# First products of two feed-forward layers by seven block products, with their input operands kept in DRAM

## The chip, the cores and the metric

The program runs on one core of a Trainium2 chip. The metric is the device time of one execution in microseconds (us); lower is better. Names used for the engines: PE is TensorE (matrix products into the eight banks of PSUM), PEld its weight loads, DVE is VectorE, ACT is ScalarE, POOL is GpSimd, SP is the engine that issues nearly all DMAs here, in one queue in program order.

## The reference

```python
def _attn_ref(q, k, v):                      # 4 batches, 8 heads, 576 tokens, 64 wide
    scores = scale * np.matmul(q, k.transpose(0, 1, 3, 2))
    ...                                      # heads 0-3: window of 32; heads 4-7: every 32nd key
    return np.matmul(attn, v).astype(np.float32)
def _moe_ref(x, w_in, w_out):                # x: 2304 x 512, w_in: 512 x 2048, w_out: 2048 x 512
    h = x @ w_in
    g = h * np.clip(h + 3.0, 0.0, 6.0) / 6.0
    return (g @ w_out).astype(np.float32)
def _moe2_ref(x, w_in, w_out):               # the same shapes, with g = h * tanh(softplus(h))
    ...
```

Attention is followed by the two layers, each on the output of the one before. The weights are given as 64-bit floats. Both layers have a first product (h = x w_in) and a second one (g w_out), of the same size.

## The kernel before, in words

**Precision.** Every FP32 operand is split into a high and a low part; a product is three matmuls (`mm3`: low weights by high data, high by low, high by high; lines 801 to 803).

**Tiles.** Everything is kept transposed: 512 features are four chunks of 128 partitions (`xh[kc]`, `xl[kc]`: high and low parts of the layer's input), tokens lie along the columns. The 2304 tokens are cut into blocks of 512, 512, 512, 256 and 512 (`BLOCKS`), the 2048 hidden features of a layer into 16 chunks of 128, and these into three groups (`GROUPS`). A step is one chunk of hidden features on one block: 4 x 3 matmuls into one bank (h), the activation out of the bank (ACT `t`, in the first layer also DVE `t`), the split into `gh` (ACT, line 332) and `gl` (POOL, line 867), then 4 x 3 matmuls into four banks (y), which collect over the steps of a group. After a group, y is added to a sum in SBUF (DVE, line 905). After the last group of layer 1 the sum is split into `xh`, `xl` again; after the last of layer 2 it goes out.

**Weights** come by DMA as 64-bit words (`raw`, 512 KB each, 64 of them) and are decoded on DVE and ACT in `decode` (lines 749 to 790), ahead of their use.

**Attention** runs in 16 pairs (4 batches x 4 pairs of heads). A pair is scores (PE, line 569), softmax (DVE, POOL, ACT), transposes (PE, lines 636 and 638), and values (PE, line 675). Pair p of a batch gives chunk p of the features. A step needs the batches that its tokens lie in.

**Order.** `Plan` is a list scheduler that runs when the program is built: every operation has a cost, a due time and a set of engines that can do it, and the result is one fixed order for each engine. Until 60 us it also puts in matmuls on zeros (line 929), to keep PE at work. While attention runs, the layers' first group is interleaved with it.

Of the kernel before, what the change touches and what calls it, by code (L numbers as in the profile page):

```python
# [31 lines left out]
BLOCKS = (512, 512, 512, 256, 512)  # L32

GROUPS = ((4, 6, 6), (6, 5, 5))

LAST_WALK = (0, 1, 2, 4, 3)


SLOTS = 8
EARLY_SLOTS = 6  # L40
EARLY_SUMS = 2

N_RAW, N_WA, N_WM, N_T, N_G = 3, 3, 2, 4, 4
N_QKV, N_E, N_PT = 2, 4, 2

# [5 lines left out]
    "att": (0, 1, 2, 3),  # L51
    "y": (4, 5, 6, 7),
    "h0": (0, 1, 2, 3),
    "h1": (0, 1, 2),
    "y0": (4, 5, 6, 7, 3, 2),
    "y1": (4, 5, 6, 7, 3),
# [5 lines left out]
START, FIRST_PACE = 42731, 3854  # L62
UNIT = 1354
MASKS_DUE = 1000

SOON = 54
# [4 lines left out]
HALF_PACE = 7747  # L71
EARLY_W, EARLY_G, EARLY_X = 9802, 9863, 14382


BIAS = {"act": -442, "dve": 4000, "pool": 0}
FIRST_BIAS = {"act": 3541, "dve": 4000, "pool": 0}
BIAS_FROM = 29872
# [11 lines left out]
LEAD = 0.8883  # L89
# [207 lines left out]
def mm3_ns(n):  # L297

    return 3 * (n + 32) / 2.4
# [7 lines left out]
def attention_then_two_ffns(ctx, tc, qkv, masks, wts, out):  # L307
# [13 lines left out]
    N = max(BLOCKS)  # L321

    blocks = [(sum(BLOCKS[:j]), n) for j, n in enumerate(BLOCKS)]
    assert sum(BLOCKS) == NT and all(sum(g) == NF for g in GROUPS)

# [15 lines left out]

    w_t = [pool.tile([P, 2, DM], F32R, name=f"w{k}") for k in range(2 * EARLY_SLOTS)]
# [3 lines left out]
    gh_t = [pool.tile([P, N], F32R, name=f"gh{k}") for k in range(N_G)]  # L346
    gl_t = [pool.tile([P, N], F32R, name=f"gl{k}") for k in range(N_G)]

    pool.tile([P, 8], F32, name="gap")
    raw_t = [pool.tile([P, DM], U64, name=f"raw{k}") for k in range(N_RAW)]  # L350
    wa_t = [pool.tile([P, DM], F32, name=f"wa{k}") for k in range(N_WA)]
    wm_t = [pool.tile([P, DM], F32, name=f"wm{k}") for k in range(N_WM)]
    all_t = pool.tile([P, N_T, N], F32, name="t")
    t_t = [all_t[:, k] for k in range(N_T)]

    early_ys = pool.tile([P, EARLY_SUMS, KC, N], F32, name="y")
    ys = [early_ys[:, j] for j in range(EARLY_SUMS)]

# [12 lines left out]
    sums, words = (x.rearrange(how) for x, how in ((early_ys, "p j a n -> p (j a n)"), (all_t, "p k n -> p (k n)")))  # L371
# [18 lines left out]
    class Record:  # L390
        pass

    steps = []
    for m in range(2):
        for g, n in enumerate(GROUPS[m]):
            walk = LAST_WALK if (m, g) == (1, len(GROUPS[1]) - 1) else range(len(blocks))
# [608 lines left out]
```

## Time and profile before

| | |
|---|---|
| median of 3 runs | 879.99 us (878.77 to 880.93) |
| the profiled execution: its own time | 879.24 us |
| the profiled execution: span of its trace | 877.4 us, mean granted PE clock 0.991 |
| PE, DVE, ACT, POOL busy | 98%, 50%, 35%, 32% of the span |
| moved by DMA | 57.12 MB |

The span is what the trace covers; 1.84 us of the execution's own time lie outside it. Busy shares are means over the span; matmuls overlap one another in the pipeline, so the time between their starts tells more than their durations.

### The profile page before, as it was taken

How to read it: one execution, taken by the hardware profiler on the slowest of the kernel's cores; microseconds unless marked ns; L12 is line 12 of the kernel's file. 1: busy time of each engine (PE TensorE's matmuls, PEld its weight loads, DVE VectorE, ACT ScalarE, POOL GpSimd, SP SyncE). 2: the span in 40 equal slices, each digit the busy share in tenths (PEclk: the TensorE clock that was granted, in tenths of full speed). 3: DMA queues.
4: the chain of work that ended last, by engine and by line, in shares of the span. 5: the costliest groups of instructions: out<-in, count | busy, mean ns of one | idle time of the engine just before them, and what ended most of it. 6: DMA issues, size and time to landing. Idle time of an engine off the chain costs nothing.

```text
span 877.4 us, 15050 instructions
## 1 busy us (share of the span) xinstructions
PE 857.9 (98%) x6326; PEld 715.6 (82%) x6326; DVE 440.9 (50%) x788; ACT 309.3 (35%) x581; POOL 279.9 (32%) x244
## 2 busy tenths in 40 slices
PE   5899999999999999999999999999999999999998
PEld 2577888888888988888888888898888898888887
DVE  5688868899321588942268960007881114110011
ACT  2566765542222233323333432334422222222221
POOL 4544542322222222334442532222322223222221
PEclk7999999999999999999999999999999999999999
DMA  8846542223000022300002220001320000010012
GB/s 263 250 141 212 156 127 93 77 92 98 22 1 1 25 73 72 96 25 1 1 25 96 72 96 1 1 1 55 114 97 1 1 1 1 0 49 25 25 48 72
DMA packets 19495, 57.12 MB, mean 65 GB/s; under 512 B 2916, under 2 KB 5604, under 8 KB 19428
## 3 DMA queue, kind: packets, MB, share of 16 engines
q1 hardware_dynamic: 18768, 56.01, 19.9%
q8 instruction: 49, 0.80, 0.4%
q10 hardware_dynamic: 660, 0.16, 0.1%
q14 instruction: 18, 0.15, 0.0%
HBM read 51.45 MB, written 4.72 MB: 64 GB/s over the span
## 4 chain that ended last, share of the span: by engine, by line
PE 93%; DMA 3%; ACT 1%; POOL 1%; DVE 1%; issue 0%; SPq 0%; ACTq 0%; POOLq 0%
PE bank L801 30%; PE bank L802 30%; PE bank L803 30%; DMA v<-in_qkv_dram 2%; PE bank L675 2%; PE bank L569 1%; PE bank L636 1%; DMA mk_str<-in_masks_dram 1%; ACT v L535 0%; ACT pt L332 0%; POOL mk_str L492 0%; POOL v L537 0%; PE bank L638 0%; POOL e L627 0%; PE bank L929 0%
## 5 line engine op out<-in xcount | busy, mean ns | idle before, releaser
L867 POOL TENSOR_TENSOR gl<-t,gh 128x512 fp32r<-128x512 f32 (+1 forms) x160 | 204.0, 1275 | 532.6 <-ACT gh L332 460.2
L801 PE MATMUL bank<-gh,w 128*128 128x512 f32 (+1 forms) x640 | 237.8, 372 | 0.0
L801 PE MATMUL bank<-xh,w 128*128 128x512 f32 (+1 forms) x640 | 237.2, 371 | 0.1
L802 PE MATMUL bank<-xl,w 128*128 128x512 f32 (+1 forms) x640 | 236.0, 369 | 0.0
L803 PE MATMUL bank<-xh,w 128*128 128x512 f32 (+1 forms) x640 | 235.8, 368 | 0.0
L802 PE MATMUL bank<-gl,w 128*128 128x512 f32 (+1 forms) x640 | 235.8, 368 | 0.0
L803 PE MATMUL bank<-gh,w 128*128 128x512 f32 (+1 forms) x640 | 235.6, 368 | 0.0
L801 PEld LDWEIGHTS bank<-xh,w 128*128 128x128 f32 x640 | 120.7, 189 | 21.2 <-DVE w L790 0.4
L802 PEld LDWEIGHTS bank<-xl,w 128*128 128x128 f32 x640 | 120.8, 189 | 20.1
L803 PEld LDWEIGHTS bank<-xh,w 128*128 128x128 f32 x640 | 120.6, 188 | 20.2
L801 PEld LDWEIGHTS bank<-gh,w 128*128 128x128 f32 x640 | 120.6, 188 | 20.2
L803 PEld LDWEIGHTS bank<-gh,w 128*128 128x128 f32 x640 | 120.5, 188 | 20.3
L802 PEld LDWEIGHTS bank<-gl,w 128*128 128x128 f32 x640 | 120.6, 189 | 19.0
L905 DVE TENSOR_TENSOR y<-bank,y 128x512 f32<-128x512 f32 (+1 forms) x80 | 49.5, 636 | 170.6 <-PE bank L803 170.3
L820 ACT ACTIVATE t<-bank 128x512 f32<-128x512 f32 (+1 forms) x80 | 44.5, 556 | 240.0 <-PE bank L803 239.9
L332 ACT CAST gh<-t 128x512 fp32r<-128x512 f32 (+1 forms) x160 | 92.7, 580 | 60.0 <-DVE t L812 39.4
L812 DVE SCALAR_TENSOR_TENSOR t<-t,bank 128x512 f32<-128x512 f32 (+1 forms) x80 | 50.5, 632 | 124.5 <-ACT t L809 124.2
L809 ACT ACTIVATE t<-bank 128x512 f32<-128x512 f32 (+1 forms) x80 | 44.5, 556 | 144.6 <-PE bank L803 144.2
L778 DVE TENSOR_SCALAR wa<-wa 128x512 uint32<-128x512 uint32 x64 | 38.8, 607 | 107.7 <-ACT w L332 107.0
L332 ACT CAST w<-wa 128x512 fp32r<-128x512 f32 x64 | 39.7, 621 | 47.6 <-DVE wa L772 24.7
L772 DVE SCALAR_TENSOR_TENSOR wa<-raw,wa 128x512 uint32<-128x512 uint32 x64 | 54.7, 855 | 0.5
L786 DVE SCALAR_TENSOR_TENSOR wm<-wm,raw 128x512 f32<-128x512 uint32 x64 | 49.7, 776 | 0.1
(53 smaller groups left out, 535.1 us busy)
## 6 DMA issues: line engine op xcount, KB each, us to landing
raw<-in_wts_dram SPq DMA_DIRECT2D x64, 512.0 KB, 3.6
qk<-in_qkv_dram SPq DMA_DIRECT2D x14, 576.0 KB, 4.9
v<-in_qkv_dram SPq DMA_DIRECT2D x14, 432.0 KB, 4.9
out_dram<-y SPq DMA_DIRECT2D x16, 256.0 KB, 2.0
y<-in_qkv_dram SPq DMA_DIRECT2D x2, 576.0 KB, 8.2
out_dram<-y SPq DMA_DIRECT2D x4, 128.0 KB
v<-in_qkv_dram SPq DMA_DIRECT2D x14, 32.0 KB, 4.8
y<-in_qkv_dram SPq DMA_DIRECT2D x1, 432.0 KB
```

What stands on the lines that cost most here:

```text
L332: nc.scalar.copy(out, src)
L772: lambda: nc.vector.scalar_tensor_tensor(ai, high, 0xC0000000, ai, ALU.bitwise_and, ALU.bitwise_or),
L778: lambda: nc.vector.tensor_scalar(ai, ai, 0xFF800000, None, ALU.bitwise_and), [o], lock=("dve",),
L786: lambda: nc.vector.scalar_tensor_tensor(rest, resti, 2.0 ** 32, low, ALU.mult, ALU.add), [o], lock=("dve",),
L801: nc.tensor.matmul(o, a[:, 1], high, start=first, stop=False)
L802: nc.tensor.matmul(o, a[:, 0], low, start=False, stop=False)
L803: nc.tensor.matmul(o, a[:, 0], high, start=False, stop=last)
L809: o = add("act", act_ns(n, True), lambda: nc.scalar.activation(t, h(), AF.Relu, bias=0.5, scale=1.0 / 6.0), [prod, free])
L812: lambda: nc.vector.scalar_tensor_tensor(t, t, 1.0, h(), ALU.min, ALU.mult), [o], frees=s.h,
L820: return add("act", act_ns(n, True), lambda: nc.scalar.activation(t, h(), AF.Mish), [prod, free], frees=s.h)
L867: lambda eng, gh=gh, gl=gl, t=t: engines[eng].tensor_tensor(gl, t, gh.bitcast(F32), ALU.subtract),
L905: lambda y=y, src=src: nc.vector.tensor_tensor(y(), src(), y(), ALU.add), [op, *before], due=due, frees=bank,
```

## The change

**Seven products.** For the first product of both layers, a unit takes two pairs of hidden chunks (`u.fs`, two at a time) and two runs of tokens of the same width (`TOKENS`: 2 x 288, 2 x 432, 2 x 432). Tokens, features and hidden chunks are each halved, and the eight block products of a 2 x 2 by 2 x 2 product become seven (Strassen's scheme in Winograd's form). The seven data operands (`PRODUCTS`: three blocks and four sums `s1` to `s4`) and the weight operands (four blocks and the differences `t1` to `t4`) are made on DVE, POOL and ACT. Each product is 2 x 3 matmuls for each of the two hidden pairs. Partial results go on collecting in a bank after a copy of it was taken: the copies (`c`, `u`, `v`) are made by ACT, and a later product in another bank is added to the copy on DVE.

**Operands in DRAM.** `xh` and `xl`, which held all split data, are gone. `xs` holds the unsplit data in SBUF (and takes the sums of y). In a layer's first group, each operand is made in one of five slots `x` (four during attention) and also written to DRAM (`kept`); the three later groups read it back by DMA.

**Groups** are now four in each layer, of two hidden pairs each, so there are 24 units (4 groups x 3 token runs x 2 layers). A unit has 84 matmuls of the first and 96 of the second product. y is added into `xs` after every unit. The planner's constants are new.

```diff
-BLOCKS = (512, 512, 512, 256, 512)
-GROUPS = ((4, 6, 6), (6, 5, 5))
+TOKENS = ((0, 288), (576, 432), (1440, 432))
+BLOCKS = (((2,), (2,), (2,), (2,)), ((2,), (2,), (2,), (2,)))
+PRODUCTS = ("a11", "a12", "s2", "s1", "s4", "s3", "a22")
+N_X, N_X_EARLY = 5, 4
     "att": (0, 1, 2, 3),
+    "h_att": (4, 5, 6, 7),
+    "y_att": (4, 5, 6, 7),
+    "h": (0, 1, 2, 3),
     "y": (4, 5, 6, 7),
-    "h0": (0, 1, 2, 3),
...
-    xh = [pool.tile([P, NT], F32R, name=f"xh{kc}") for kc in range(KC)]
-    xl = [pool.tile([P, NT], F32R, name=f"xl{kc}") for kc in range(KC)]
+    x_t = [pool.tile([P, 2, 2, WIDE], F32R, name=f"x{k}") for k in range(N_X_EARLY)]
+    xs = [pool.tile([P, NT], F32, name=f"xs{kc}") for kc in range(KC)]
...
+    def x_operands(u, i, due):
...
+        if not u.first:
+            o = add(
+                "dma", dma_ns(16 * P * n) * 1.2, lambda: nc.sync.dma_start(full().bitcast(F32), kept[u.m, u.p, i]), [x_kept[u.m, u.p, i], *old],
+            )
+            return slot, [[o], [o]], use
...
+                elif kind == "s3":
+                    o = also(lambda eng, x=x, f=f: sub(eng, f(), x(0, 0), x(1, 0)), [*deps, *old_f])
+                    reads = [o]
...
+                ops = split(n, hi, lo, f, [o], old, due)
...
+        o = x_kept[u.m, u.p, i] = add(
+            "dma", dma_ns(16 * P * n) * 1.2, lambda: nc.sync.dma_start(kept[u.m, u.p, i], full().bitcast(F32)), [*parts[0], *parts[1]], due=due + 8000,
+        )
...
+        for i in range(7):
+            x_slot, x_parts, x_use = x_operands(u, i, due - EARLY_X)
+            piece, block, step = W_FOR[i]
+            for fp in u.fs:
+                w_slot, w_ready = in_ready[m, fp]
+                bank = (a, c, a, a, a, b, b)[i][fp]
+                start = i in (0, 1, 5)
+                for q in range(2):
...
+                    deps.extend({2: u.out.get(("c", fp), []), 3: u.out.get(("u", fp), []), 4: u.out.get(("v", fp), []), 6: u.out.get(("c22", fp), [])}.get(i, []))
+                    o = prods[fp, i, q] = add("pe", cost, emit, deps, due=due, bank=bank if start and q == 0 else None)
...
+                elif i in (0, 2, 3):
+                    kind = {0: "c", 2: "u", 3: "v"}[i]
...
+                    o = add(None, copy_ns(n, True), lambda eng, tile_of=tile_of, psum=psum: copy(eng, tile_of(), psum()), [o, *old])
+                    u.out[kind, fp] = [o]
...
+                elif i in (5, 6):
...
+                    o = add(
+                        "dve", dve_ns(n), lambda tile_of=tile_of, psum=psum: nc.vector.tensor_tensor(tile_of(), psum(), tile_of(), ALU.add),
+                        [o, *u.out[kind, fp]], frees=b[fp] if i == 6 else None,
+                    )
```

**What stands on PE in layer 1, before.** The next rows are from PE's order in the middle of layer 1: a step's four chunks of `xh`, `xl` into one bank (h), then matmuls of earlier steps (`gh`, `gl`) into y banks, and so on in turn. A wait in brackets is on another engine's semaphore.

```order
L801 MATMUL bank0_61<-xh3_84,w8_77 128x512
L802 MATMUL bank0_61<-xl3_88,w8_77 128x512
L803 MATMUL bank0_61<-xh3_84,w8_77 128x512
L801 MATMUL bank7_68<-gh2_91,w5_74 128x512 [waits Activation_49]
L802 MATMUL bank7_68<-gl2_95,w5_74 128x512 [waits Pool_49]
L803 MATMUL bank7_68<-gh2_91,w5_74 128x512
L801 MATMUL bank1_62<-xh0_81,w10_79 128x512 [waits DVE_49]
```

**The same place in the program after the change:** the end of the first product of a unit of width 432 in layer 1. Only the first matmul of each run of six is shown, with the first two of the second product that follow (`win0` and `win1` are the weights of the two hidden pairs).

```order
L949 MATMUL bank1_62<-x0_73,win0_69 128x432 [waits DMAHW2_49,Activation_49]
...
L949 MATMUL bank2_63<-x0_73,win1_70 128x432 [waits Activation_49]
...
L949 MATMUL bank1_62<-x1_74,win0_69 128x432 [waits DMAHW3_49,Activation_49]
...
L949 MATMUL bank2_63<-x1_74,win1_70 128x432 [waits Activation_49]
...
L949 MATMUL bank0_61<-x2_75,win0_69 128x432 [waits DMAHW5_49,DVE_49]
...
L949 MATMUL bank0_61<-x3_76,win0_69 128x432 [waits DMAHW6_49,DVE_49]
...
L949 MATMUL bank4_65<-gh0_77,wout2_2454 128x432
L950 MATMUL bank4_65<-gl0_85,wout2_2454 128x432 [waits Pool_49]
```

What moved: runs of six matmuls on the same bank now return after six others, and each return waits for a copy (ACT) or a sum (DVE) of what the bank held; such waits did not exist inside a first product.

**SP's queue in layer 1, before,** held nothing but weight loads. After attention its rows are these three over and over (three `raw` buffers).

```order
L749 DMA raw2_100<-in_wts_dram 128x512 [waits DMAHW1_49,DMAHW6_49,DVE_49,Activation_49]
L749 DMA raw0_98<-in_wts_dram 128x512 [waits DMAHW2_49,DMAHW7_49,DVE_49,Activation_49]
L749 DMA raw1_99<-in_wts_dram 128x512 [waits DMAHW0_49,DMAHW3_49,DVE_49,Activation_49]
L749 DMA raw2_100<-in_wts_dram 128x512 [waits DMAHW1_49,DMAHW4_49,DVE_49,Activation_49]
L749 DMA raw0_98<-in_wts_dram 128x512 [waits DMAHW2_49,DMAHW5_49,DVE_49,Activation_49]
```

**SP's queue after the change,** in the second group of layer 1: loads of kept operands stand between the weight loads, which wait for the decode of an earlier weight.

```order
L883 DMA x3_76<-kept0_1_0_124 128x4x432 [waits DMAHW6_49,PE_49]
L883 DMA x4_2456<-kept0_1_1_125 128x4x432 [waits DMAHW7_49,PE_49]
L883 DMA x0_73<-kept0_1_2_126 128x4x432 [waits PE_49]
L883 DMA x1_74<-kept0_1_3_127 128x4x432 [waits DMAHW3_49,DMAHW1_49,PE_49]
L883 DMA x2_75<-kept0_1_4_128 128x4x432 [waits DMAHW4_49,DMAHW2_49,PE_49]
L772 DMA raw0_97<-in_wts_dram 128x512 [waits DVE_49,Activation_49]
L772 DMA raw1_98<-in_wts_dram 128x512 [waits DVE_49,Activation_49]
L772 DMA raw2_99<-in_wts_dram 128x512 [waits DMAHW5_49,DVE_49,Activation_49]
L883 DMA x3_76<-kept0_1_5_129 128x4x432 [waits DMAHW6_49,PE_49]
```

What moved: a unit's last two operands now stand behind three weight loads that wait for DVE and ACT.

## Rows read from the trace of the kernel before

**Rows 1.** The page: busy time, share of the span and instructions of each engine.

```profile
PE 857.9 (98%) x6326; PEld 715.6 (82%) x6326; DVE 440.9 (50%) x788; ACT 309.3 (35%) x581; POOL 279.9 (32%) x244
```

**Rows 2.** Windows: start:end, us, then busy us of each engine, PE clock, DMA, GB/s.

```profile
0.00:50.00 50.00, 35.80 (x884) 22.92 (x885) 33.26 (x79) 19.84 (x47) 23.80 (x42) 0.86 0.77 237
50.00:100.00 50.00, 48.35 (x977) 38.20 (x976) 42.34 (x89) 35.67 (x70) 24.66 (x19) 1.00 0.56 172
100.00:150.00 50.00, 50.00 (x927) 41.05 (x926) 39.37 (x80) 29.03 (x60) 20.53 (x16) 1.00 0.44 136
...
600.00:640.00 40.00, 40.00 (x178) 33.12 (x177) 32.01 (x60) 16.45 (x30) 14.05 (x8) 1.00 0.30 99
```

**Rows 3.** PE's order in time: start and us between starts of matmuls, 512 and 256.

```profile
500.01 0.39 PE L801 MATMUL bank<-gh,w 128*128 128x512 f32 x1
500.24 0.39 PE L802 MATMUL bank<-gl,w 128*128 128x512 f32 x1
...
440.07 0.28 PE L801 MATMUL bank<-gh,w 128*128 128x256 f32 x1
440.19 0.28 PE L802 MATMUL bank<-gl,w 128*128 128x256 f32 x1
```

**Rows 4.** Groups of PE and PEld instructions by shape: one of six alike each.

```profile
L803 PE MATMUL bank<-gh,w 128*128 128x512 f32 x512 | 199.4, 389 | 0.0
L803 PE MATMUL bank<-gh,w 128*128 128x256 f32 x128 | 36.2, 283 | 0.0
...
L803 PEld LDWEIGHTS bank<-gh,w 128*128 128x128 f32 x640 | 120.5, 188 | 20.3
```

**Rows 5.** The chain that ended last, in time: start, us, what (attention).

```profile
45.37 1.18 PE bank L675 x72
53.61 1.32 PE bank L675 x72
75.63 1.18 PE bank L675 x72
114.33 1.18 PE bank L675 x72
125.62 0.59 PE bank L636 x4
132.66 0.98 PE bank L569 x62
147.00 1.18 PE bank L675 x72
148.18 0.43 PE bank L801
```

**Rows 6.** Order in time at the end of the program.

```profile
872.71 1.50 DVE L905 TENSOR_TENSOR y<-bank,y 128x256 f32<-128x256 f32 x4 [6.86 <-PE bank L803]
873.47 0.28 PE L803 MATMUL bank<-gh,w 128*128 128x256 f32 x1
```

**Rows 7.** Order in time around handovers between PE, ACT and POOL.

```profile
563.25 0.39 PE L801 MATMUL bank<-gh,w 128*128 128x512 f32 x1
563.51 0.60 ACT L820 ACTIVATE t<-bank 128x512 f32<-128x512 f32 x1 [4.19 <-PE bank L803]
...
32.99 0.37 ACT L332 COPY pt<-bank 128x256 f32<-128x256 f32 x1 [3.03 <-PE bank L636]
33.51 0.65 PE L636 MATMUL bank<-mk,e 128*128 128x128 f32 x2 [0.45 <-ACT pt L332]
```

**Rows 8.** Groups of ACT and DVE instructions by shape: busy us, mean ns.

```profile
L332 ACT COPY y<-bank 128x512 f32<-128x512 f32 x32 | 18.3, 590 | 5.5 <-PE bank L803 4.8
L332 ACT COPY y<-bank 128x256 f32<-128x256 f32 x8 | 2.6, 391 | 0.0
...
L905 DVE TENSOR_TENSOR y<-bank,y 128x512 f32<-128x512 f32 x64 | 43.5, 689 | 162.7 <-PE bank L803 162.4
L905 DVE TENSOR_TENSOR y<-bank,y 128x256 f32<-128x256 f32 x16 | 6.0, 422 | 7.9 <-PE bank L803 7.9
...
L772 DVE SCALAR_TENSOR_TENSOR wa<-raw,wa 128x512 uint32<-128x512 uint32 x64 | 54.7, 855 | 0.5
```

**Rows 9.** The page: DMA issues, KB each, median us to landing.

```profile
raw<-in_wts_dram SPq DMA_DIRECT2D x64, 512.0 KB, 3.6
```

More of the change, by code (lines that the diff above doesn't have):

```diff
@@ L415, in attention_then_two_ffns @@
+    whole = [min(-(-(t0 + 2 * n) // S), B) for t0, n in TOKENS]
+    t = START
+    for u in units:
+        u.at = t
+        cost = len(u.fs) * 2 * mm3_ns(u.n)
+        u.one, u.two = 7 * cost, 8 * cost
+        t += u.one + u.two
+        if u.early and u.p + 1 < len(TOKENS):
+            t += (whole[u.p + 1] - whole[u.p]) * NPAIR * UNIT / len(BLOCKS[0][0])
     mk_load, pairs, last_use = {}, {}, {}
@@ L584, in masked @@
             )
-        s_op = add("pe", 900, scores, [src.qk], bank=both)
+        s_op = add("pe", 900, scores, [src.qk, *e_free], bank=both)
         s_op.count = 4 * (4 * NB + 2)
@@ L711, in attention_then_two_ffns @@
         x_ready.append(ready)
-        first = next(s for s in steps if whole[s.j] > b)
-        pace = FIRST_PACE if b == 0 else (first.at - next(s for s in steps if whole[s.j] > b - 1).at) / NPAIR
+        j = next(j for j, w in enumerate(whole) if w > b)
+        first = next(u for u in units if u.p == j)
+        if b == 0:
+            pace, last = FIRST_PACE, first.at
+        else:
+            before = next(u for u in units if u.p == j - 1).at
+            share = whole[j] - whole[j - 1]
+            pace = (first.at - before) / NPAIR / share
+            last = first.at - (whole[j] - 1 - b) * NPAIR * pace
@@ L727, in attention_then_two_ffns @@
-    t = 1e12
-    for k in order[::-1]:
-        t = w_due[k] = min(w_due[k] - EARLY_W, t - HALF_PACE)
-    w_ready, w_ops = {}, []
-    def decode(k):
-        m, c, half = order[k]
-        raw, a, rest = raw_t[k % N_RAW], wa_t[k % N_WA], wm_t[k % N_WM]
+    halves = [(m, fp, k) for m in range(2) for fp in range(NF // 2) for k in range(4)]
+    h_due, t = {}, 1e12
+    for u in units:
+        for i, fp in enumerate(u.fs):
+            for k in range(4):
+                at = u.at if k < 2 else u.at + u.one
+                h_due.setdefault((u.m, fp, k), at + i * u.one / 7)
@@ new lines, in attention_then_two_ffns, with pitch, mm3 @@
+    x_second = {}
+    def pitch(n):
+        return WIDE if n == N else n
+    for p, (t0, n) in enumerate(TOKENS):
+        x_done[0, p] = [
+            [op for b in range(t0 // S, -(-(t0 + 2 * n) // S)) for op in x_ready[b][kc]] for kc in range(KC)
+        ]
+    def mm3(o, high_w, low_w, high, low, first, last):
+        nc.tensor.matmul(o, low_w, high, start=first, stop=False, skip_group_check=True)
+        nc.tensor.matmul(o, high_w, low, start=False, stop=False, skip_group_check=True)
+        nc.tensor.matmul(o, high_w, high, start=False, stop=last, skip_group_check=True)
@@ new lines, in attention_then_two_ffns, with take @@
+    t_count, t_free = 0, {}
+    s_count, s_free = dict.fromkeys("cuv", 0), {}
+    g_free = {}
+    y_sums, y_count = {}, 0
+    S_EARLY = {"c": 2, "u": 2, "v": 2}
+    s_owner = {k: {} for k in "cuv"}
+    def take(kind, u):
+        early = S_EARLY[kind]
+        many = early if u.early else early + 1
+        k = s_count[kind] % many
+        s_count[kind] += 1
+        old = s_owner[kind].get(k)
+        return (kind, k), old if old is not None else ([closing] if k >= early else [])
+    opened = [None]
@@ L927, in attention_then_two_ffns @@
+    for u in units:
+        build(u)
     cleared = add("dve", 520, lambda: nc.vector.memset(zeros, 0.0), due=0)
```

536 lines of the change are left out of this document (324 added, 212 removed).

## Prediction

> **What bounds the kernel now.** I read the page first: PE is busy 98% of the span, no other engine above 50% [rows 1]. A busy PE can still be slack, so next come the windows: after 50 us it is busy in all of nearly every stretch at a granted clock of 1.00, while DVE reaches 32 of 40 us in a stretch of weight decoding [rows 2]. Last, the starts of matmuls: in the layers they follow one another without a hole, 0.227 us apart at width 512 and 0.120 us at width 256 [rows 3]. Both are (width + 32) columns at 2.4 GHz: 544/2.4 = 227 ns, 288/2.4 = 120 ns. So a matmul costs its columns and 32 more.
>
> The layers' matmuls are 6 x 512 at width 512 and 6 x 128 at 256 [rows 4]: 3072 x 0.2267 + 768 x 0.120 = 788.5 us of the 877.4. The rest is attention. The last values of the sixteenth pair end at 148.18 [rows 5]. By PE's program order, 291 of the layers' matmuls stand before them, worth 64.0 us, so 724.4 us are left; 148.2 + 724.4 = 872.6, and the last matmul starts at 873.47 [rows 6]. From there on PE loses 1 us in all; 3.8 us of sums and output follow to the end of the span. The time is therefore the moment at which attention ends, plus the matmuls still to come, plus whatever PE waits in between. I make the sum for the changed kernel in this form.
>
> **The matmuls.** 24 units of 180 matmuls, 8 units at width 288 and 16 at 432: 1440 x 320/2.4 = 192.0 us and 2880 x 464/2.4 = 556.8 us, 748.8 us in all, **39.7 us less**. Without the 32 columns the seven-for-eight saving would be 46.1 us (half of 737.3, an eighth); 480 more matmuls at 13.3 ns take 6.4 back. Neither width is in the trace; both lie between or beside the two measured ones, and the same line fits both of those.
>
> A rule of the Trainium skill speaks against narrow tiles: "TensorE: Matmul & The Clock Gate", section "Back-to-back issue gap", says that the spacing in a stream of weight loads and matmuls is set by both. A weight load lasts 188 ns here [rows 4]; were that a floor, 1440 matmuls of 133 ns would cost 188 ns and the saving would turn into a loss of about 39 us. The trace does not agree: at width 256 matmuls start every 120 ns [rows 3], well below the load's 188. The same section gives width/2.4 + 2.5 ns for a matmul alone, by which the saving would be about 45 us; the measured 227 ns at 512 decides against it.
>
> **Attention's end.** In PE's new order only 48.4 us of the layers' matmuls stand before the last values, so 700.4 us follow them. Unit 1 needs batches 1 and 2 whole, so PE has little but unit 0 to fill with until pair 12. I take three pieces.
> - Pair 4 ends at 46.5 before [rows 5]. I keep that: the DMA queue is the same up to there, and DVE's instruction count up to that pair's softmax is 54 after 57.
> - Pairs 5 to 12 took 69 us (45.37 to 114.33, [rows 5]), with 39.4 us of the layers' matmuls among them. Now there are 14.4 us of those, and a pair takes PE 1.18 (values), 0.98 (scores) and about 0.7 (0.59 for four of its six transposes) [rows 5], 2.9 us: PE needs 37.6 us. DVE, the busiest other engine here (42 of 50 us, [rows 2]), has 89 instructions in place of 123: 69 x 89/123 = 50 us. ACT has 91 in place of 94, and was busy only 36 of 50. I take 50 us. Bounds: 38 (PE alone) and 67 (by ACT's count; the clock granted in the first 50 us was 0.86 with thin PE work [rows 2], and such a stretch would end here too).
> - Pairs 13 to 16: PE has 33.2 us of layers and 11.6 of attention, 44.8; DVE has 83 instructions at 69/123 us, 47. I take 48.
>
> So attention ends at 46.5 + 50 + 48 = 145 us (129 to 162). It ends little earlier although PE has 15.6 us less to do before it: that is where a good part of the gain goes. DRAM copies of the operands (7 x 0.88 MB in a unit of width 432) share the queue with loads of q, k and v. Two units' copies, the batches and weights are some 26 MB in 100 us, 260 GB/s, while DMA moved 237 GB/s at a share of 0.77 [rows 2], 308 at full share. That fits, not by much, and the upper bound has to hold it.
>
> **Handovers inside a product.** This is new and unlike anything before: a run of six matmuls returns to its bank only after ACT's copy or DVE's sum, and the cover is the other column's run of six: 6 x 193 = 1.16 us at width 432, 0.80 us at 288. From the rows: ACT starts 0.26 us after the next matmul began (563.25 to 563.51), and PE starts 0.15 us after an ACT copy's end (33.36 to 33.51) [rows 7]. A copy out of PSUM lasts 0.39 us at 256 and 0.59 at 512, a DVE sum 0.42 and 0.69 [rows 8]; along the line, 0.53 and 0.61 at 432, 0.42 and 0.46 at 288. So a handover by ACT is 0.26 + 0.53 + 0.15 = 0.94 us against 1.16 (0.83 against 0.80 at 288), by DVE 1.02 (0.87). With free engines nothing is lost at 432, and about 2 us in all eight narrow units. A unit has four by ACT and two by DVE. If each of them found the longest instruction ahead (DVE 0.86 us, [rows 8]; ACT about 0.6), a wide unit would lose 4 x 0.4 + 2 x 0.7 = 3 us, a narrow one 4.5 us; as what one column waits is cover for the other I halve it: 42 us. Between 2 and 42 I go by the engines' shares: counted from the new order and at today's mean duration, DVE has 1115 instructions x 0.56 = 624 us and ACT some 900 x 0.53 = 478, 0.73 and 0.56 of the time. Met at a random moment a busy engine costs half an instruction: 0.56 x 0.3 = 0.17 us on ACT, less than the 0.22 spare; 0.73 x 0.35 = 0.26 us on DVE, twice the spare. About 0.4 us for a wide unit, 0.6 for a narrow one: 16 x 0.4 + 8 x 0.6 = **11 us**.
>
> **What stays hidden.** Reading operands back: 16.5 MB a group and 4.2 MB of weights in 93.6 us of PE work are 221 GB/s, 0.72 of the 308. A 512 KB load lands in 3.6 us [rows 9], a 0.88 MB one in about 5 by the same rate; four of five slots are ahead of PE, 2.3 us each, and during a unit's second product (18.6 us) they fill. If that cover went, each late operand would cost up to 5 us. Making operands in layer 2's first group (40 instructions a unit on DVE, POOL and ACT) has a whole unit's time; the y sums go into `xs` off the path. At layer 1's last group every result is needed one unit or more later. The tail is as before.
>
> **Sum,** against the profiled execution: 145 + 700.4 + 1 + 11 + 3.8 = 861.2 us of span, and 879.24 - 877.4 = 1.84 us outside: 863.0. The profiled execution lies 0.75 us under the median of the runs, which changes nothing at this accuracy. **863 us.** The ends of all terms give 129 + 700.4 + 1 + 2 + 3.8 + 1.8 = 838 and 162 + 700.4 + 1 + 42 + 3.8 + 1.8 = 911. No change means within 0.3%, 877.4 to 882.6 us, about what measurement can tell.
>
> **Rivals.**
> - *Nearly the whole gain.* DVE is no limit in attention, pairs 5 to 12 take PE's 38 us and the rest 45, and handovers cost 2 to 4 us: 838 to 850. For it: DVE's count there fell by 28%. Against it: DVE was at 42 of 50 us [rows 2] and remains the next bound.
> - *Handovers eat it (slower).* DVE and ACT work through their queues in a fixed order, and DVE's decoding takes 32 of 40 us at times [rows 2]. If the six handovers mostly queue behind one instruction, units lose about 1.8 us (the 42 us) and the time is 863 + 31 = 894. It decides against the change when a unit loses over 1.1 us on average: (879.2 - 852.0)/24.
> - *Operands late from DRAM (slower).* In SP's queue a unit's last two operands stand behind three weight loads that wait for decoding. If DVE runs 5 us late there, the slots' lead is gone; 1 to 2 us a unit in 18 reading units is 18 to 36 us: 881 to 899. For it: the queue is in order. Against it: 0.72 of the rate, and weights themselves are decoded well ahead.
> - *No saving in the columns.* The weight load bounds narrow matmuls: 1440 x (188 - 133) ns, 79 us more, 942. The 120 ns rows exclude it but for one in a hundred.
>
> **Chances.** Forecast's own case (850 to 877): 0.55. Nearly the whole gain: 0.22. Handovers: 0.12. Late operands: 0.07, a quarter of that still under 877. Saving spent to within 0.3%: 0.03 and an edge of the others. That makes faster 0.78, same 0.06, slower 0.16. The range 845 to 887 leaves out about one in ten on each side; the likeliest case alone is 850 to 877.
>
> **What would show it.** Matmuls 193 ns apart at 432 and 133 ns at 288, and 748.8 us by count. The last values end near 145 us, PE thin from 50 to 95 us and full after it. After 150 us PE waits 0.1 to 0.7 us for ACT's copies `c`, `u`, `v` and DVE's sums, some 11 us in all, more in narrow units. DMA share 0.6 to 0.75 throughout, no PE wait on operands `x`. I am wrong if attention ends after 160 us or before 132, if waits at handovers exceed 25 us, or if PE waits for loads from `kept`.

## The result and the profile after

The changed kernel takes **867.86 us** (median, 866.41 to 870.77) beside 880.46 us for the kernel before in the same session: ratio 0.986, 95% interval 0.983 to 0.989. Forecast were 863.0 us and 845 to 887. The profiled execution of the changed kernel took 866.41 us, 864.6 of them span.

The page (busy time, share of the span and instructions of each engine), the counterpart of [rows 1]:

```profile
PE 839.3 (97%) x6830; PEld 787.0 (91%) x6830; DVE 591.8 (68%) x1118; ACT 424.0 (49%) x895; POOL 220.0 (25%) x240
```

VectorE grew by 34% and ScalarE by 37%; the forecast went by 624 and 478 us for them, measured are 592 and 424. The windows (start:end, us, busy us of each engine, PE clock, DMA share, GB/s), the counterpart of [rows 2]:

```profile
0.00:50.00 50.00, 40.35 (x926) 24.23 (x928) 32.71 (x74) 23.42 (x54) 27.25 (x45) 0.90 0.83 248
50.00:100.00 50.00, 40.09 (x1083) 32.93 (x1076) 41.67 (x87) 36.87 (x86) 25.41 (x27) 1.00 0.83 265
100.00:150.00 50.00, 49.01 (x822) 44.94 (x823) 43.68 (x79) 38.91 (x89) 22.89 (x20) 1.00 0.59 192
```

In the stretch from 50 to 100 us PE is idle for 9.9 us; before it was idle for 1.7 there. VectorE is no busier than it was, and the DMA share went from 0.56 to 0.83.

The chain that ended last, in time (start, us, what), the counterpart of [rows 5]:

```profile
49.58 1.18 PE bank L690 x72
...
123.38 1.18 PE bank L690 x72
...
148.66 1.18 PE bank L690 x72
149.84 0.39 PE bank L949
```

L690 is now the line of the values. Pair 4 ends at 50.8 us (49.58 + 1.18) and pair 16 at 149.84. From there to the end, the order in time (start, us, what, idle time before and its releaser) answers to [rows 3, 6, 7]:

```profile
205.20 0.29 PE L951 MATMUL bank<-x,win 128*128 128x288 f32 x1
206.74 0.44 PE L949 MATMUL bank<-x,win 128*128 128x432 f32 x1 [1.25 <-DVE t L1002]
...
680.63 0.29 PE L951 MATMUL bank<-x,win 128*128 128x288 f32 x1
681.36 0.43 PE L949 MATMUL bank<-x,win 128*128 128x432 f32 x1 [0.43 <-DMA x<-kept]
...
702.17 0.35 PE L949 MATMUL bank<-x,win 128*128 128x432 f32 x1
702.36 0.35 PE L950 MATMUL bank<-x,win 128*128 128x432 f32 x1
...
831.46 0.36 PE L951 MATMUL bank<-gh,wout 128*128 128x432 f32 x1
831.66 0.29 PE L949 MATMUL bank<-x,win 128*128 128x288 f32 x1
...
861.22 0.29 PE L951 MATMUL bank<-gh,wout 128*128 128x288 f32 x1
861.55 0.46 DVE L1106 TENSOR_TENSOR xs<-bank,xs 128x288 f32<-128x288 f32 x1 [0.73 <-PE bank L951]
```

These rows hold what happens after attention. The first two pairs of rows are PE's only waits worth the name, 1.4 and 0.6 us; no other matmul started late by more than about 0.1 us. Neither is at one of the six handovers inside a product: the first ends with the activation's step on VectorE (`t`), the second with a load. The stretch of 432 columns from 702.17 to 831.66 has no wait at all, yet its 657 matmuls take 197.1 ns each (129.49 us / 657), where the forecast has 464/2.4 = 193.3.

Copies and sums of a product (groups by shape: busy us, mean ns), beside [rows 8]:

```profile
L334 ACT COPY v<-bank 128x432 f32<-128x432 f32 x32 | 16.7, 521 | 13.2 <-PE bank L951 12.5
...
L1067 DVE TENSOR_TENSOR v<-bank,v 128x432 f32<-128x432 f32 x32 | 19.4, 605 | 8.8 <-PE bank L951 8.6
```

The forecast has 0.53 and 0.61 us for these two; measured are 0.52 and 0.605.

**Where the span's 12.8 us come from** (877.4 to 864.6), with the kernel before taken as in the prediction: matmuls by the line -39.7; attention ends 1.7 us later (148.18 to 149.84) although 15.7 us fewer of the layers' matmuls stand before it (48.4 in place of 64.0), together +17.3; spacing and waits of PE after it, 711.5 us (149.84 to 861.36) for 700.4 us by the line, 11.1 lost in place of 1, +10.1; the tail, 3.3 in place of 3.8, -0.6. Sum, before rounding: -12.8.

So two things had to be explained: 11.1 us lost by PE in a part of the program where it hardly waits, and 17 us lost near the attention.

### The profile page after: what moved, and what is told of

Read it like the earlier page. It is cut to its first block, busy times and chain, and to the rows that moved or that the text cites. A ratio compares the mean times of both kernels' runs of the same rounds, so it can differ in the third digit from the quotient of the medians.

```text
span 864.6 us, 17057 instructions
## 1 busy us (share of the span) xinstructions
PE 839.3 (97%) x6830; PEld 787.0 (91%) x6830; DVE 591.8 (68%) x1118; ACT 424.0 (49%) x895; POOL 220.0 (25%) x240
## 4 chain that ended last, share of the span: by engine, by line
PE 91%; DMA 4%; POOL 1%; DVE 1%; issue 1%; ACT 1%; ACTq 0%; SPq 0%; POOLq 0%
PE bank L949 29%; PE bank L950 28%; PE bank L951 28%; PE bank L1127 2%; PE bank L690 2%; PE bank L584 1%; DMA v<-in_qkv_dram 1%; DMA qk<-in_qkv_dram 1%; DMA x<-kept 1%; PE bank L651 1%; DMA mk_str<-in_masks_dram 1%; POOL x L755 1%; POOL f L893 0%; DVE t L1002 0%; DVE f L893 0%
## 5 line engine op out<-in xcount | busy, mean ns | idle before, releaser
L949 PE MATMUL bank<-gh,wout 128*128 128x432 f32 (+1 forms) x768 | 260.4, 339 | 0.6 <-ACT xs L334 0.6
L950 PE MATMUL bank<-gl,wout 128*128 128x432 f32 (+1 forms) x768 | 259.5, 338 | 0.4 <-issue 0.4
L951 PE MATMUL bank<-gh,wout 128*128 128x432 f32 (+1 forms) x768 | 259.2, 337 | 0.0
L949 PE MATMUL bank<-x,win 128*128 128x432 f32 (+1 forms) x672 | 229.9, 342 | 2.4 <-DVE t L1002 1.3
L950 PE MATMUL bank<-x,win 128*128 128x432 f32 (+1 forms) x672 | 227.0, 338 | 1.6 <-POOL x L755 1.6
L951 PE MATMUL bank<-x,win 128*128 128x432 f32 (+1 forms) x672 | 226.7, 337 | 0.0
L1106 DVE TENSOR_TENSOR xs<-bank,xs 128x432 f32<-128x432 f32 (+1 forms) x144 | 80.2, 557 | 110.0 <-PE bank L951 109.3
L755 POOL TENSOR_TENSOR gl<-t,gh 128x432 fp32r<-128x432 f32 (+1 forms) x65 | 67.8, 1047 | 328.8 <-ACT gh L334 198.8
L949 PEld LDWEIGHTS bank<-gh,wout 128*128 128x128 f32 x768 | 144.5, 188 | 5.8 <-ACT xs L334 0.9
L950 PEld LDWEIGHTS bank<-gl,wout 128*128 128x128 f32 x768 | 144.7, 188 | 5.4 <-issue 0.6
L951 PEld LDWEIGHTS bank<-gh,wout 128*128 128x128 f32 x768 | 144.6, 188 | 4.5
L949 PEld LDWEIGHTS bank<-x,win 128*128 128x128 f32 x672 | 126.4, 188 | 8.4 <-DVE t L1002 1.5
L950 PEld LDWEIGHTS bank<-x,win 128*128 128x128 f32 x672 | 126.5, 188 | 6.5 <-POOL x L755 2.3
L951 PEld LDWEIGHTS bank<-x,win 128*128 128x128 f32 x672 | 126.4, 188 | 3.8
L755 DVE TENSOR_TENSOR gl<-t,gh 128x432 fp32r<-128x432 f32 (+1 forms) x127 | 78.1, 629 | 44.0 <-ACT gh L334 42.0
L334 ACT CAST gh<-t 128x432 fp32r<-128x432 f32 (+1 forms) x192 | 96.2, 511 | 14.8 <-DVE t L1002 12.5
```

The lines of the kernel that those rows point to most:

```text
L334: nc.scalar.copy(out, src)
L755: lambda eng: engines[eng].tensor_tensor(lo(), src(), hi().bitcast(F32), ALU.subtract),
L949: nc.tensor.matmul(o, low_w, high, start=first, stop=False, skip_group_check=True)
L950: nc.tensor.matmul(o, high_w, low, start=False, stop=False, skip_group_check=True)
L951: nc.tensor.matmul(o, high_w, high, start=False, stop=last, skip_group_check=True)
L1106: "dve", dve_ns(n), lambda y=y, src=src: nc.vector.tensor_tensor(y(), src(), y(), ALU.add),
```

## Experiments

### Widths alone, twice

A kernel of its own: 60 matmuls of each width in a row, from constant tiles, with one weight load each as in the layers. The second one has other orders of the widths.

```diff
+WIDTHS = (256, 272, 288, 304, 320, 352, 384, 400, 416, 424, 432, 440, 448, 464, 480, 496, 512)
...
+    for n in (512,) + WIDTHS:
+        for _ in range(20):
+            mm3(n, count % 8, count % 4)
```

This is e1; e5 has another line for the widths.

```diff
+WIDTHS = (512, 496, 480, 464, 448, 440, 432, 424, 416, 400, 384, 320, 288, 256, 432, 288, 432, 448, 384, 448)
```

> A stream of matmuls alone, 60 at each of 17 widths with a new weight load each, no DMA and no other engine at work; it computes nothing of the reference. Theory W (width 432 itself costs more than its 432 + 32 columns): spacing at 432 is 196 to 198 ns here too, while 256, 288 and 512 are at 120, 133 and 227. Theory T (traffic: operand loads or the other engines slow PE's reads): 193.3 ns at 432, all widths on the line (width + 32)/2.4.

> The stream of matmuls alone once more (it computes nothing of the reference), in another order of widths: 512 down to 256, and then 432, 288, 432, 448, 384, 448. Theory, the width itself sets the extra time: mean spacing in e1 was 195.9 ns at 432 and 206.6 ns at 448 against 193.3 and 200.0 on the line (width + 32) / 2.4, and 384 and 512 stood within 0.5 ns of it. Every segment at 432 should give 195.5 to 196.5 ns and every one at 448 205.5 to 207.5 ns, first or last in the stream, with 384 between the two segments at 448 at 173 to 174 ns. Rival, the extra time belongs to the place in the stream (how long the engine has run): then the excess moves to other widths, 432 comes out near 193.3 ns in some segments, and the 384 late in the stream is above 175 ns.

Measured spacings (time between starts over a segment, by its matmuls; good to some 0.3 ns, since the rows give starts to 0.01 us), in ns, with the line (width + 32)/2.4 in the last row ("later" are the segments behind 256 in e5, whose 512 stands at the start of the stream and is left out):

```
width   256    288    384    400    416    424    432    440    448    512
e1    119.8  131.7  173.4  180.0  188.3  193.4  195.9  199.8  206.6  227.1
e5    120.0  131.7  173.7  180.0  186.7  193.5  195.8  200.0  202.7      -
later        131.5  173.3                       195.7         202.7
                                                196.2         206.6
line  120.0  133.3  173.3  180.0  186.7  190.0  193.3  196.7  200.0  226.7
```

Two rows of e5 in time, the first start at 432 and that of the segment behind it, from which 195.8 comes (11.75 us / 60):

```profile
98.24 0.36 PE L32 MATMUL bank<-x,w 128*128 128x432 f32 x1
...
109.99 0.36 PE L32 MATMUL bank<-x,w 128*128 128x424 f32 x1
```

And the first and the last start of the last segment, at 448, from which 206.6 comes (12.19 us / 59):

```profile
231.87 0.36 PE L32 MATMUL bank<-x,w 128*128 128x448 f32 x1
...
244.06 0.37 PE L34 MATMUL bank<-x,w 128*128 128x448 f32 x1
```

At 432 the excess belongs to the width and not to the place in the stream: it is the same in three places of e5, with 288 between. With no other engine at work 432 is 2.5 ns above the line; up to 400 and at 512 the line holds within 0.5 ns, except that 288 lies 1.6 ns under it. That is 7 us over 2,880 matmuls. At 448 the width alone does not settle it: the same tiles took 202.7 ns twice in e5 and 206.6 in its last segment, as in e1, so only one of three came out at the 205.5 to 207.5 expected. Width and tiles don't set it there by themselves; what else does is open.

### Units of 256, 448 and 448

```diff
-TOKENS = ((0, 288), (576, 432), (1440, 432))
+TOKENS = ((0, 256), (512, 448), (1408, 448))
...
```

> Token runs of 256, 448 and 448 in place of 288, 432 and 432 (one buffer fewer for the copies c, and q, k, v buffers moved 64 columns so that the wider tiles fit); the line gives the same 748.8 us for the matmuls. Theory W (432 is a bad width, 448 is on the line at 200.0 ns): about 9 us of spacing come back, 858 us. Theory T (traffic slows all wide matmuls by 2%): 2880 x 4 ns stay, 867 to 870 us. In both cases unit 0 has 11% less work to fill attention with, worth up to 3 us more.

Measured: 870.58 us, ratio 0.987 (0.985 to 0.990), and no wait of over about 0.1 us after attention. The 448 columns took 204.1 ns on average, 4.1 above the line and between the two values that they took alone: 11.0 us lost again. No gain, since 448 is off the line too.

### No loads of the kept operands after layer 1's second group

```diff
-    lambda: nc.sync.dma_start(full().bitcast(F32), kept[u.m, u.p, i])
+    lambda: nc.sync.dma_start(full().bitcast(F32), kept[u.m, u.p, i]) if (u.m, u.g) == (0, 1) else None
```

> Leaves out the loads of kept operands in every group after the second one of layer 1, so that PE multiplies stale operands there; the plan and every other instruction stay. DMA traffic after 250 us falls from some 220 GB/s to weights and stores. Theory hidden (loads cost PE nothing): the one wait for a load (0.4 us) goes, time within 2 us of the changed kernel's 867.9. Theory T (traffic slows matmuls): spacing at 432 falls from 197 to 193 ns in the groups without loads, some 7 us less, 861.

Measured: 868.61 us, ratio 0.985 (0.983 to 0.987): nothing gained, so the loads after layer 1's second group are hidden, and the late-operand rival falls. The spacing at 432 is 197.1 ns as in the changed kernel, so it does not come from traffic either. What is more, single stretches repeat: the six longest of this width, in their order, take 198.1, 196.3, 197.4, 196.0, 197.9 and 197.1 ns in both kernels. Something fixed in the program makes them differ.

### Each copy of a product twice

```diff
...
-                    o = add(None, copy_ns(n, True), lambda eng, tile_of=tile_of, psum=psum: copy(eng, tile_of(), psum()), [o, *old])
+                    o = add(None, copy_ns(n, True), lambda eng, tile_of=tile_of, psum=psum: [copy(eng, tile_of(), psum()) for _ in range(2)], [o, *old])
...
```

> Every copy c, u, v out of a bank is made twice into the same tile, the order of all engines unchanged: a handover by ACT grows by one copy, from 0.94 to about 1.45 us at width 432 (cover 1.16) and from 0.83 to 1.23 at 288 (cover 0.80). Theory cover (handovers cost nothing now because they fit under the other column's run): the two handovers in a row of a unit stick out by 0.3 to 0.5 us each, 24 units x 2 x 0.4 = about 19 us more, 880 to 890. Theory slack (the plan interleaves enough second-product matmuls that cover does not matter): within 4 us of 867.9.

Measured: 884.06 us, ratio 1.003 (1.001 to 1.005), 16.2 us more. PE now waits where the forecast looked for waits, as in this row in time:

```profile
210.91 0.37 PE L949 MATMUL bank<-x,win 128*128 128x288 f32 x1 [0.70 <-ACT v L334]
```

After its last values (end 155.4) this kernel loses 23.3 us, 12 more than the changed one, in 82 starts late by over 0.05 us. The rest is a later end of attention, at a granted clock of 0.90 from 50 to 100 us where the changed kernel has 1.00, so that part is not shown to come from the copies. So the cover is real and thin: one copy of 0.52 us fits under six matmuls of the other column, two don't.

### Four units of 288

```diff
-TOKENS = ((0, 288), (576, 432), (1440, 432))
+TOKENS = ((0, 288), (576, 288), (1152, 288), (1728, 288))
...
-LAST_WALK = (1, 2, 0)
+LAST_WALK = (1, 2, 3, 0)
```

> The changed kernel with four units of 288 columns per half (1152 of 2304 tokens each pair of units) in place of 288, 432, 432, so that every unit needs one batch of the attention only. The layers have 5,760 matmuls, 768.0 us by the line and 761.5 us at the 132.2 ns that 288 shows in the trace, against 748.8 and about 758 us. Theory, the unit that has to wait for both batches costs the time near the attention: two units (48 us) can run on the first batch alone, so 8 to 15 us more of matmuls lie before the last values at about 150 us, the extra time of width 432 is gone, and the time is 850 to 862 us. Rival, what limits the stretch to 150 us is the attention with its copies and its transfers: the same 48 us lie before the last values, and the time is 864 to 872 us. Second rival, narrow units leave too little work to cover a handover: stalls of 0.5 to 1.5 us in most of 32 units, 880 to 910 us.

(There are four batches of four pairs each; the second unit needs the second batch, pair 8, which the expectation words wrongly.) Measured: 879.54 us, ratio 0.999 (0.997 to 1.001). The expected mechanism happened and bought nothing. Its values (instructions by line: duration min/median/max, first and last start), and its window from 50 to 100 us:

```profile
L690 PE MATMUL bank<-pt,v x1008: 219/219/291, 26.0 to 166.2; 64*64 64x32 f32 x168
...
50.00:100.00 50.00, 37.22 (x816) 32.57 (x815) 45.40 (x96) 34.36 (x86) 30.30 (x34) 0.86 0.77 265
```

62.4 us of the layers' matmuls stood before the last values in place of 48.4, 14.0 more, and the last values ended at 166.5, 16.6 us later. After that 705.6 us of matmuls by the line took 705.7: waits of 3.7 us, and a spacing of 132.7 ns, below the line's 133.3, that gives them back. A wait of 0.1 us a unit is all that narrow handovers cost here (3.7 us over some 29 units). The gain failed because attention ended later by more than the work put before it. Part of that is the clock: it was 0.86 from 50 to 100 us where the changed kernel has 1.00, which is at most 7 us of PE's work (0.14 x 50). So at least 9 of the 16.6 us came with the added work; how the rest divides is not shown.

### No transfers of the operands

Stores to and loads from `kept` are left out; later groups multiply whatever the slots hold (the fifth slot, which would stay empty, is filled once).

```diff
...
-    lambda: nc.sync.dma_start(full().bitcast(F32), kept[u.m, u.p, i])
+    lambda: None
...
-    lambda: nc.sync.dma_start(kept[u.m, u.p, i], full().bitcast(F32))
+    lambda: None
```

> The changed kernel without any transfer of its block operands: they are neither stored to DRAM nor loaded, later groups multiply what the slots hold. Matmuls, copies and their order stay. Theory A, the stores of the first operands (576 and 864 KB each, at 0.83 of the queues in 50 to 100 us) hold the attention's loads back: the last values start at 138 to 144 us in place of 148.6 and the time falls by 5 to 10 us, to 857 to 863. Theory B, the attention is late by PE's and VectorE's own work: the last values start at 147 to 153 us, and the time is 865 to 869 us. In both, the spacing at width 432 stays at 196 to 198 ns, since in e3 it did not go with the traffic.

Measured: 861.07 us, ratio 0.977 (0.975 to 0.979): 6.8 us less, in theory A's range. The last values start at 144.1, at its edge, and end at 145.3:

```profile
144.06 1.25 PE L691 MATMUL bank<-pt,v 64*64 64x32 f32 x72
```

The DMA issues from 45 to 110 us (KB each, median us from issue to landing), first in the changed kernel:

```profile
kept<-x SPq DMA_DIRECT2D x7, 576.0 KB, 6.9
v<-in_qkv_dram SPq DMA_DIRECT2D x8, 432.0 KB, 5.6
```

and without the operands' transfers:

```profile
v<-in_qkv_dram SPq DMA_DIRECT2D x8, 432.0 KB, 3.9
```

The loads of v land 1.7 us sooner without the stores, and `DMA v` is 8.7% of the chain in this stretch in place of 15.0%. Of the 6.6 us of span 4.5 are the earlier end of attention and 2.1 lie after it, where the waits at 205 and 681 us are gone; the spacing at 432 stays at 197.0 ns. Pair 4 ends at 50.2 (50.8 with the transfers), pairs 5 to 12 take 48.5 us (52.4), and pairs 13 to 16 take 46.6 in both. With a granted clock of 1.00 from 50 to 150 us in both, the transfers cost 4 us in pairs 5 to 12. With e3, which left only later loads out and gained nothing, that is shown for the transfers as a whole, not for the stores of layer 1 by themselves.

### No making of operands in layer 1

The sums of blocks and the splits of the first group are left out, the slots hold a constant, written by 16 copies on VectorE (5.4 us) before 7 us (the expectation counts the layers from 0).

```diff
...
+    if u.m == 0:
+        x_reads.setdefault((u.m, u.p), []).extend(deps)
+        parts.append(deps)
+        continue
...
```

> The changed kernel without the making of the block operands in layer 0: the sums of blocks and the splits into high and low words that the first group makes from the attention's results are left out (some 16 us of ScalarE, 22 us of GpSimd and 25 us of VectorE before 150 us), and the slots hold a constant. The stores and loads of the operands, all matmuls and all copies of products stay. Theory, the making of operands and the attention's own passes share VectorE, ScalarE and GpSimd, and that is why the attention ends at 150 us though 15 us fewer matmuls of the layers stand before it: the last values start at 133 to 142 us in place of 148.6, and the time is 852 to 861 us. Rival, the pace is set by the loads of the attention's inputs and by the banks: the last values start at 146 to 152 us, and the time is 865 to 870 us.

Measured: 871.86 us, ratio 0.989 (0.985 to 0.992), above both ranges; the last values end at 152.6. The window from 50 to 100 us:

```profile
50.00:100.00 50.00, 40.60 (x1032) 34.27 (x1036) 37.74 (x78) 32.92 (x77) 16.48 (x16) 0.93 0.80 259
```

VectorE, ScalarE and GpSimd have 3.9, 4.0 and 8.9 us less to do than in the changed kernel, and PE is as idle as it was (9.4 us). Pairs 5 to 16 took 102.7 us, 99.0 in the changed kernel. The granted clock was 0.93 in this window where the changed kernel has 1.00, which is at most 3.5 us of PE's work, so they were no faster at a like clock either: my theory that these engines hold the attention back falls. The DMA share stays at 0.80.

### Three units of 384

```diff
-TOKENS = ((0, 288), (576, 432), (1440, 432))
+TOKENS = ((0, 384), (768, 384), (1536, 384))
...
-START, FIRST_PACE = 43020, 5332
+START, FIRST_PACE = 64348, 5332
...
```

> The changed kernel with three units of 384 columns in place of 288, 432 and 432. The sum of the matmuls by the line (width + 32) / 2.4 is the same, 748.8 us, but 384 stood on the line in e1 and e5 (173.3 to 173.7 ns), so the 9 us of extra spacing at 432 go. The first unit now needs the results of 8 of the 16 attention pairs in place of 4, the second 12, the third 16. Theory, only the matmuls that fit before the attention's end count: with the first 8 pairs undisturbed by the layers, and 30 to 45 us of the layers' matmuls (the first unit and part of the second) before last values at 140 to 150 us, the time is 855 to 866 us. Rival, the late start leaves TensorE idle: under 25 us of the layers' matmuls before the last values, and 870 to 885 us.

Measured: 875.28 us, ratio 0.992 (0.989 to 0.994). Neither story holds whole: 55.1 us of the layers' matmuls stood before the last values, more than either said, but these ended at 171.8. The windows:

```profile
0.00:50.00 50.00, 36.58 (x859) 21.52 (x860) 26.19 (x59) 20.18 (x47) 18.51 (x37) 0.86 0.73 214
50.00:100.00 50.00, 42.14 (x852) 29.49 (x852) 37.02 (x75) 29.36 (x62) 18.57 (x17) 0.84 0.70 226
```

The granted clock was 0.86 and 0.84 where the changed kernel has 0.90 and 1.00, at much the same busy time of PE (36.6 and 42.1 us, 40.4 and 40.1 there); what made it fall is not shown. And 384, which was on the line alone, took 175.1 ns here, 7 us over 4,001 matmuls. So in the kernel something is added to the width's own time at 384 too, and at 512, as the next run shows.

### Units of 256, 512 and 384, and then 32 bytes

```diff
-TOKENS = ((0, 288), (576, 432), (1440, 432))
-WIDE = 448
+TOKENS = ((0, 256), (512, 512), (1536, 384))
+WIDE = 512
...
```

> The changed kernel with units of 256, 512 and 384 columns, in the order of the tokens (after 4, 12 and 16 pairs, as now). All three widths stood on the line in e1 and e5 (120.0, 226.7 and 173.5 ns), the sum stays at 748.8 us. The wider tiles cost buffers: one slot of operands, one of activations, and one each of the copies c, u and v fewer. Theory, the extra time at 432 is a matter of its width: the part after the last values loses under 3 us by spacing in place of 9, the last values stay at 147 to 153 us, and the time is 857 to 863 us. Rival, the missing buffers turn into waits of TensorE, for copies or operands, of over 6 us in all: 866 to 880 us.

Measured: 871.57 us, ratio 0.988 (0.986 to 0.991). No waits to speak of (1.3 us after attention), but in long stretches the 512 columns took 230.9 ns on average, where the kernel before has 226.7 [rows 3], and 9.4 us were lost again; the last values ended at 160.7. The time lies in the rival's range, but not by the rival's reason: the buffers are not it.

This is where the theory of the width alone fell. I put each start in the trace beside the operands' addresses in the compiled program. The spacing goes with the address of the columns and that of the next matmul's weights, modulo 64 bytes (mean ns, matmuls):

```
                      same modulo 64 bytes    32 bytes apart
changed, 432          195.8  (1440)           198.4  (1189)
e2, 448               203.1  (1441)           205.2  (1185)
e10, 512              229.4  (600)            233.4  (585)
e9, 384               173.9  (2126)           176.6  (1866)
```

In the kernel before every operand of the layers stands at 0 modulo 64. Its two empty tiles `gap` and `late_gap`, of 32 and 832 bytes, go with the change; since then the early tiles (those of the main pool, there from the start) stand at 32, the late ones, which come after attention, at 0. The next two kernels move the main pool by 32 bytes and change nothing else.

```diff
+    pool.tile([P, 8], F32, name="gap")
     dp = ctx.enter_context(tc.tile_pool(name="kept", bufs=1, space=bass.MemoryType.DRAM))
```

> The changed kernel with 32 bytes more at the end of its main pool, which moves the early weight, operand and activation tiles from 32 to 0 modulo 64 bytes; the late ones stand at 0 already, and nothing else changes. In the changed kernel a matmul of 432 columns took 195.8 ns where its columns and the next weights stand at the same address modulo 64 bytes and 198.4 ns where they differ by 32; in e10 512 columns took 229.4 and 233.4 ns, and in the kernel before, where all of them stand at 0, 226.7. Theory, the place of the two modulo 64 bytes sets the extra time: every pair at 432 takes 195.3 to 196.2 ns whichever tile it reads, the mean falls from 197.1 to 195.8, 3.3 us over 2,753 matmuls, and the time is 863 to 866 us. Rival, the late tiles are slow for another reason (where they lie): the 2.6 ns between early and late weights stay, and the time is 866 to 870 us.

> e10 with the same 32 bytes. Theory: 512 columns take 226.5 to 227.0 ns as in the kernel before and in e5 (230.9 in e10), 384 take 173.2 to 173.8 (174.9), so that the part after the last values loses 0.5 to 2.5 us in place of 9.3, and the time falls from 871.6 to 861 to 866 us, if the last values stay near 160 us. Rival, the address is not it: spacing and time stay as in e10, 869 to 873 us.

Measured: 866.32 us, ratio 0.981 (0.978 to 0.984), and 865.09 us, ratio 0.980 (0.977 to 0.983). The stretch that stands above for the changed kernel, now in e11:

```profile
705.22 0.35 PE L950 MATMUL bank<-x,win 128*128 128x432 f32 x1
...
833.84 0.30 PE L950 MATMUL bank<-x,win 128*128 128x288 f32 x1
```

128.62 us / 657 = 195.8 ns, in place of 197.1. The six stretches listed under e3 lie at 195.7 to 196.0, where they were at 196.0 to 198.1 before, and 195.8 is what 432 takes alone. After its last values e11 needs 708.4 us in place of 711.5 for the same matmuls. The theory holds for 432 and takes 3.1 us, as expected. The whole of e11's time came out 1.5 us lower only, 0.3 us above the theory's range and inside the rival's, with overlapping intervals: in its profiled execution attention ended at 155.1. The window from 50 to 100 us, in the changed kernel, in e3 and in e11, in this order (all three have the same order of work there):

```profile
50.00:100.00 50.00, 40.09 (x1083) 32.93 (x1076) 41.67 (x87) 36.87 (x86) 25.41 (x27) 1.00 0.83 265
50.00:100.00 50.00, 39.99 (x1048) 32.97 (x1049) 40.09 (x83) 34.65 (x81) 25.71 (x27) 0.94 0.79 249
50.00:100.00 50.00, 39.59 (x1093) 32.67 (x1093) 39.23 (x80) 36.19 (x85) 26.14 (x27) 0.96 0.75 240
```

Attention ends at 149.8, 153.7 and 155.1 in these three, and the granted clock goes with it: 1.00, 0.94 and 0.96 here (and 0.97 in e11 from 100 to 150, where the other two have 1.00). It does so from run to run as well: the four runs of the changed kernel have a mean clock of 0.994 at 866.4 to 868.1 us and 0.986 at 870.8. So the spacing is judged here by the part after attention, where the clock is 1.00.

In e12 the part after attention loses 3.5 us by the line in place of 9.4, and in long stretches 512 columns take 228.7 in place of 230.9, 384 columns 174.1 in place of 174.9. Better, though not the 226.7 and 173.5 that the address alone would give (the expectation names e5 for 512, but the figure is the kernel before's, and 227.1 in e1): 2 ns at 512 stay open. The time fell by 6.5 us, as expected; in the profiled executions 5.9 us of the fall lie after attention and 6.3 before its end (154.4 for 160.7), and the second part is not shown to come from the 32 bytes. By its median e12 is the fastest of the kernels here that leave nothing out.

## Why the prediction came out right, step by step

**Right.** The change is faster by 1.4%, by the mechanism of the forecast: seven products save matmuls (40 us by the line, 30 as measured), a good part goes back near the attention, and some 11 us are lost after it, by another cause than forecast. The four rivals didn't happen. Doubling the copies (e4) shows that the handover rival had its place and lay one copy away; leaving loads out (e3) shows that late operands cost next to nothing. One of the prediction's own signs of being wrong did appear, a PE wait for a load from `kept`, once, for 0.6 us.

**The matmuls, mis-sized.** "Neither width is in the trace; both lie between or beside the two measured ones, and the same line fits both of those": so 748.8 us. Measured means give 2880 x 197.1 + 1440 x 132.4 ns = 758.3 us, 9.5 more: 7.2 by the width itself (2.5 ns each), 3.7 by the place modulo 64 bytes (1.3 ns), and 1.3 given back by the narrow ones. The step that failed is the straight line between two measured widths: both had been measured with all operands at one place modulo 64 bytes, and the line passes under 432 even then (195.8, e5 and e11). The saving is 30, not 40 us. The narrow matmuls were no trouble: 132.4 ns where 133.3 was forecast.

**Handovers, mis-sized in the other direction.** 11 us between bounds of 2 and 42; measured are two waits of 2.0 us in all, and neither is at such a handover. The durations at 432 were right to 0.01 us, and with them 0.94 us against a cover of 1.16. What failed is the queueing estimate, half an instruction for a busy engine at a random moment: the copies and sums were in time for nearly every product. The order on PE helped: of the returns to a bank counted in the compiled program, 23 of 42 in narrow units and 21 of 84 in wide ones have more than the six matmuls between that the forecast took as cover. In e6, with the cover at its thinnest, the waits came to 0.1 us a unit where 0.6 had been forecast for narrow ones. The two errors nearly cancel, 11.1 us lost after attention for 12 forecast: the sum was right there by luck, for a wrong reason.

**Attention, 149.84 for 145,** inside 129 to 162. Pairs 5 to 12 and 13 to 16 took 52.4 and 46.6 us for 50 and 48: pair 12 ends at 103.2 (its values start at 101.97). The step that was short is "Pair 4 ends at 46.5 before. I keep that": it ended at 50.8, and the operands' transfers are not the reason, since without them (e7) it ended at 50.2, at the same DMA share of 0.83 in the first 50 us (0.77 before; 0.6 to 0.75 was forecast throughout). Pair 1 is late already, 33.2 us for 28.5. What differs on PE there is the number of matmuls on zeros: the windows of these instructions alone (PE and PEld), before and after, are

```profile
0.00:50.00 50.00, 12.95 (x18) 3.75 (x18) 0.86 0.77 237
0.00:50.00 50.00, 23.24 (x38) 8.61 (x38) 0.90 0.83 248
```

In the chain up to 52 us they have 33.2% after the change, 4.0% before. Whether they hold the first pairs back no run here tests.

Pairs 5 to 12 are where the transfers cost 4 us (e7: 48.5 us). That VectorE sets the pace there, from which the 50 us came, is not shown: with 3.9 us less to do for it (e8) these pairs were no faster, also allowing for its lower clock. So the term came out near for a reason that stays open, and with it some 13 of the 17 us that go back near the attention. It is not the making of operands (e8), and more matmuls that could run did not help (e6). One profiled execution doesn't settle a few microseconds here, since attention's end moves with the granted clock (149.8, 153.7 and 155.1 us in the changed kernel, e3 and e11).

**The tail** took 3.3 us for 3.8.

## What to carry to other kernels

When an operand's tiles are laid out anew, look at where columns and weights lie modulo 64 bytes, and at the spacing of matmuls by tile before you look for waits: a loss with no wait in it doesn't show in any table of idle time. Measure a new width by itself; a line through two widths was wrong by 1.3% at a third. Before two traces are compared, put the granted clock of the same stretch beside each: here shifts of attention's end by 4 to 5 us went with it, as large as what the experiments were to show. And a sum that comes out right deserves the same check of its terms as one that does not.

## What the runs showed of the hardware

A matmul of 432 columns took 195.8 ns where columns and next weights stood at the same address modulo 64 bytes and 198.4 where they were 32 apart; at 512 229.4 and 233.4, at 448 203.1 and 205.2, at 384 173.9 and 176.6; at 288 next to no difference (132.4 and 132.2). That the loading of weights has a part in the spacing of matmuls is what the Trainium skill says ("TensorE: Matmul & The Clock Gate", section "Back-to-back issue gap": spacing is set by both the weight load and the matmul, pipelined); the trace agrees in so far as the place of the weights alone moves it, here by 1.0 to 1.7%. Widths from 424 to 480 were 2.4 to 3.5 ns above (width + 32)/2.4 in e5 even at one place modulo 64 bytes (448 in its last stretch 6.6), those up to 416 were not, nor was 512 in e1. PE's granted clock was 0.84 to 0.86 over the first 100 us in e9, a mean of its two levels of 1.2 and 2.4 GHz, with PE busy for 79 of them; from 50 to 100 us in the changed kernel it was 1.00 with 40 of 50.
